# Attention and expert layers in one program: the weight conversion moved into six named slots, and the score chunks in another order

## The chip, the cores and the metric

The kernel runs on one core of one Trainium2 chip. The metric is the device time of one execution in microseconds (us). Engines are named as in the profile: PE (TensorE matmul), PEld (its weight load), DVE (VectorE), ACT (ScalarE), POOL (GpSimd), SP (SyncE, which issues the transfers here).

## What is computed

Attention with a causal softmax and a linear memory, mixed by a gate, and then four matrix products:

```python
scores = scale * np.matmul(q, k.transpose(0, 1, 3, 2))      # B, H, S, D = 4, 8, 576, 64
scores = np.where(causal, -1000000000.0, scores)
a = np.exp(scores - scores.max(-1, keepdims=True))
a /= a.sum(-1, keepdims=True) + 1e-09
local = np.matmul(a, v)
q_p = phi(q)                                                # elu(q) + 1
mem_out = einsum(q_p, M_prev) / (einsum(q_p, z_prev) + 1e-06)
x = (g * mem_out + (1 - g) * local)                         # g = sigmoid(beta); to 2304 x 512
out = ((x @ w1) * (x @ w2) @ w3) @ w_out                    # w* arrive as float64
```

## The kernel before

**Pairs and batches.** Two heads of one batch are a pair; there are 16 pairs, four to a batch. `pair_step(p, F)` does a pair: it walks through the table `ORDER` and calls what each word names. `mt` transposes the memory's query, `t1` to `t5` and `th` transpose the softmax of the pair (`t_mm`, with an eviction by ACT at L265), `mm` and `pv` form the sums of memory and P.V in PSUM (`mem_mm`, `pv_mm`), and `fin` (L292 on ACT, L293 on DVE) copies them out as the high and low half of x. In the same walk the next pair p + 1 is prepared: `ss` makes its scores (`s_all`), `e4` to `e0` exponentiate its chunks (`s_exp`, L215 on ACT), `n4`, `n3`, `n2` multiply them by the gate over the row sum (`s_norm`, L224 on DVE), and `ma`, `mb`, `mc` prepare the memory's query (L137 to L158; L145 and L158 run on POOL). `lv`, `lqn`, `lq` issue loads on SP.

**Chunks.** The 576 rows of scores are five chunks, 0 to 4, of 64, 128, 128, 128, 128 queries; chunk c needs 64, 192, 320, 448 or 576 keys (`KE`). `s_all` writes chunk 4 (512 columns, and 64 more in the next bank) and chunk 3 into four PSUM banks of the pool `ps_t`, and chunks 2 and 1 into the tile `x`, which has one buffer of two banks and is also the tile of P.V's sums. `s_red` (L181, DVE) adds the mask, writes the scores to the tiles `sm` and finds the row maximum. Chunk 0 of both heads is one matmul (L190, `s_mm0`) into a fifth bank of `ps_t`, thus into the first of the four that is free again.

**Filling work.** At each `F` of `ORDER` a slot of filling work is issued: `F.slot()` steps a generator until its share is reached. During the first batch that is `w_gen`, the product of w3 and w_out (L427, 64 matmuls, each of two passes in the trace), whose results are evicted by L432 and L419. From the second batch on it is `moe_gen` of the batch before: L477 (x with w1 and w2, evicted in turn by ACT L483 and DVE L486, then L488 and L489 make the two halves of h) and L497 (h with the product of w3 and w_out).

**Weight conversion.** The weights arrive as 64-bit floats. Forty jobs convert them to 32 bit: load on SP (L388 for w3 and w_out, L303 for w1 and w2), `scale` on ACT (L314), `join` on DVE (L318, L319), and for the last sixteen also `split` (L326 on ACT, L327 on POOL). `conv_tick()` issues one step: the scale of job k, the join of job k - 1, the split of job k - 2. The loads of w1 and w2 share three buffers. `F.slot()` calls it before its filling work, twice per slot in the first 13 slots and once after, where `tick_ok()` allows it:

```python
for _ in range(self.ticks if self.n > SLOTS else 2):
    if tick[0] <= NJ + 1 and tick_ok():
        conv_tick()
```

In the program this gives two ticks before the first slot, 4 to 15 over the six slots before the first pair, 16 to 19 in pair 0, 20 to 25 in pair 1 (22 to 25 of them in the softmax slots at the end), 26 to 31 in pair 2, and 32 to 41 in the first five slots of pair 4. What stands in one engine's queue in the end is set by a scheduler that may move an instruction ahead of others of its engine; instructions under `tc.high_priority` go early.

Of the kernel before, what the change touches and what calls it, by code (L numbers as in the profile page):

```python
# [16 lines left out]

ORDER = (  # L20
    "lv mt t1 F "
    "lqn t2 th F "
    "t3a t3b F "
    "t4a F "
    "t4b t5 F "
    "mm pv ma F "
    "fin F "
    "ss lq mb F "
    "F "
    "e4 mc F "  # L30
    "n4 e3 F "
    "n3 F "
    "e2 e1 e0 n2 F "
).split()


# [5 lines left out]
def attention_moe_kernel(  # L42
# [14 lines left out]
    B, H, D, _, S = qkt.shape  # L57
    DM = H * D
    NF = w12.shape[0]
    NC = DM // 128  # L60
# [127 lines left out]
    def s_mm0(p):  # L188
        x = bank()
        nc.tensor.matmul(x[:, 0:64], lhsT=qd, rhs=raw_t[p][:, 1, 0:64], start=True, stop=True)  # L190
        s_red(p, 0, 0, x[:, 0:64], 0, 64)

    def s_all(p):
        t = raw_t[p]
        lay = []
        for a in range(2):
            lay.append([bank(), bank()])
        xx = ps_x.tile([128, 1024], F32, tag="x", name="sx")
        red = []
        for i, o, c, lo, hi in ((0, 0, 4, 0, 512), (1, 0, 4, 512, 576), (1, 64, 3, 0, 448), (2, 0, 2, 0, 320), (2, 320, 1, 0, 192)):  # L200
            for a in range(2):
                y = xx[:, 512 * a + o:512 * a + o + hi - lo] if i == 2 else lay[a][i][:, o:o + hi - lo]
                r = slice(64 * a, 64 * a + 64)
                nc.tensor.matmul(y, lhsT=t[r, 0, 128 * c - 64:128 * c + 64], rhs=t[r, 1, lo:hi], start=True, stop=True)  # L204
                red.append((c, a, y, lo, hi))
        for c, a, y, lo, hi in red:
            s_red(p, c, a, y, lo, hi, lo == 0)
        s_mm0(p)

    def s_exp(p, c):  # L210
        for a in range(2 if c else 1):
# [165 lines left out]
    def tick_ok():  # L377
        k = tick[0]
        if 12 <= k < 24:
            return w_done[0] >= (k - 8) // 2 - 3  # L380
        return k < 12 or k < limit[0] and (k < 32 or w_done[0] == NF)
# [28 lines left out]
    def conv_upto(k):  # L410
        while tick[0] <= k + (1 if k < 24 else 2):
            conv_tick()
# [103 lines left out]


    class Fill:
        def __init__(self, gen, total, slots, wait=0, lead=1.0, ticks=1):
            self.lead, self.ticks = lead, ticks  # L520
            self.wait = wait
            self.gen, self.total, self.slots = gen, total, slots
            self.spent, self.n, self.live = 0.0, 0, True

        def slot(self):
            self.n += 1
            for _ in range(self.ticks if self.n > SLOTS else 2):
                if tick[0] <= NJ + 1 and tick_ok():
                    conv_tick()
            goal = self.lead * self.total * max(0, self.n - self.wait) / (self.slots - self.wait)  # L530
            while self.live and self.spent < goal:
                self.step()
# [7 lines left out]
        def finish(self):  # L540
            while self.live:
                self.step()

    SLOTS = sum(t[0] == "F" for t in ORDER)

    def pair_step(p, F):
        nx = p + 1 < NP
        ops = dict(
            mt=(1, lambda: mem_t(p)),
            lqn=(nx, lambda: load_qn(p + 1)),  # L550
            lv=(1, lambda: load_v(p)),
            t4a=(1, lambda: t_mm(p, "4a")),
            t4b=(1, lambda: t_mm(p, "4b")),
            t3a=(1, lambda: t_mm(p, "3a")),
            t3b=(1, lambda: t_mm(p, "3b")),
            t2=(1, lambda: t_mm(p, "2")),
            t1=(1, lambda: t_mm(p, "1")),
            th=(1, lambda: t_mm(p, "h")),
            t5=(1, lambda: t_mm(p, "5")),
            ss=(nx, lambda: s_all(p + 1)),  # L560
            e4=(nx, lambda: s_exp(p + 1, 4)),
            e3=(nx, lambda: s_exp(p + 1, 3)),
            e2=(nx, lambda: s_exp(p + 1, 2)),
            e1=(nx, lambda: s_exp(p + 1, 1)),
            e0=(nx, lambda: s_exp(p + 1, 0)),
            n3=(nx, lambda: s_norm(p + 1, 2, 4)),
            n2=(nx, lambda: s_norm(p + 1, 4, 9)),
            n4=(nx, lambda: s_norm(p + 1, 0, 2)),
            lq=(p + 2 < NP, lambda: load_qk(p + 2)),
            mm=(1, lambda: mem_mm(p)),  # L570
            pv=(1, lambda: pv_mm(p)),
            fin=(1, lambda: fin(p)),
            ma=(nx, lambda: mem_a(p + 1)),
            mb=(nx, lambda: mem_b(p + 1)),
            mc=(nx, lambda: mem_c(p + 1)),
        )
        for t in ORDER:
            if t[0] == "F":
                F.slot()
            elif ops[t][0]:  # L580
                ops[t][1]()

# [31 lines left out]
        nc.vector.tensor_copy(out=gis[:, :, 2 * k:2 * k + 2], in_=gp)  # L614
    for a in range(2):
        nc.vector.tensor_copy(out=gis[64 * a:64 * a + 64, :, 8], in_=gp[64 * a:64 * a + 64, :, a])
    s_exp(0, 4)
    conv_tick()
    conv_tick()
    s_norm(0, 0, 2)  # L620
    F.slot()
    for c in (3, 2, 1):
        s_exp(0, c)
        F.slot()
    s_exp(0, 0)
    s_norm(0, 2, 9)
    F.slot()
    load_qk(1)
    mem_a(0)
# [46 lines left out]
```

## Time and profile before

| | us |
|---|---|
| median of 3 runs (lowest, highest) | 582.26 (581.95, 583.43) |
| the profiled execution | 583.85 |
| its span, first to last instruction | 582.1 |
| PE busy in the span | 553.6 |
| DVE, ACT, POOL busy | 277.1, 275.8, 127.4 |

The stages, in us from the span's start: scores of pair 0 to 10; product of w3 and w_out alone to 28; pair 0 to 57, pair 1 to about 81, pair 2 to about 106, pair 3 to 131, then twelve pairs of about 31 us with the expert layers as filling, and the last batch's expert layers alone at the end. The trace is read by engine: a row has the start, the duration, the line, the tiles (out<-in) and, in square brackets, how long the engine stood idle before it and what ended that. A PE that is busy is not always at its full rate: the granted clock has two levels, 1.2 and 2.4 GHz, and a stretch's mean tells how much of it ran at the lower one.

### The profile page before, as it was taken

The numbers are of one execution on the slowest core, as the hardware profiler recorded it, in microseconds if no ns is written. First come the engines' busy times: TensorE is split into PE (matmuls) and PEld (weight loads), VectorE is DVE, ScalarE is ACT, GpSimd is POOL, SyncE is SP. The second block draws the span as 40 slices with busy tenths as digits, with TensorE's granted clock in tenths as the row PEclk, the third lists the DMA queues.
The fourth block names the chain that finished last, engine by engine and source line by source line (L and its number), as shares of the span: only waits on it lengthen the run. The fifth ranks groups of instructions, "written<-read, shape, count | busy, mean of one in ns | idle before, by whom it ended". The sixth has DMA issues, their size and how long they took to land.

```text
span 582.1 us, 9285 instructions
## 1 busy us (share of the span) xinstructions
PE 553.6 (95%) x3440; PEld 436.8 (75%) x3440; DVE 277.1 (48%) x878; ACT 275.8 (47%) x723; POOL 127.4 (22%) x153
## 2 busy tenths in 40 slices
PE   4999879898999999999999999999999999999997
PEld 2354435456888888878887889697979897998995
DVE  6986996837562627262626263524525260111111
ACT  5565876448554445545554555443626363120220
POOL 1101263114613032303230313012130321121220
PEclk9899989798999999999999999999999999999999
DMA  7992554513020211131202120311103000000001
GB/s 288 423 353 91 179 192 147 167 56 102 29 63 21 92 35 58 34 95 42 64 28 83 47 66 29 93 59 37 59 28 101 24 2 1 37 1 20 18 1 54
DMA packets 23069, 48.31 MB, mean 83 GB/s; under 512 B 6896, under 2 KB 13040, under 8 KB 21488
## 3 DMA queue, kind: packets, MB, share of 16 engines
q1 hardware_dynamic: 23024, 47.72, 24.3%
q8 instruction: 27, 0.44, 0.3%
q14 instruction: 18, 0.15, 0.1%
HBM read 43.00 MB, written 4.72 MB: 82 GB/s over the span
## 4 chain that ended last, share of the span: by engine, by line
PE 74%; ACT 6%; DVE 5%; issue 3%; DMA 1%; POOL 1%; SPq 0%; POOLq 0%; ACTq 0%
PE m L477 32%; PE m L497 17%; PE s L234 7%; PE x L281 6%; ACT sm L215 5%; PE s L204 3%; PE m L427 2%; PE x L272 2%; DVE sm L181 1%; PE x L164 1%; DVE wp L319 1%; DVE sm L224 1%; PE sx L204 1%; DMA wst<-w 1%; DVE wp L318 1%
## 5 line engine op out<-in xcount | busy, mean ns | idle before, releaser
L477 PE MATMUL m<-xs,wsp 128*128 128x288 f32 x1536 | 224.5, 300 | 4.0 <-ACT a L483 4.0
L477 PEld LDWEIGHTS m<-xs,wsp 128*128 128x128 f32 x1536 | 208.0, 189 | 6.4 <-ACT a L483 5.4
L489 POOL TENSOR_TENSOR ht<-a,ht 128x288 fp32r<-128x288 f32 (+2 forms) x96 | 57.1, 607 | 246.4 <-ACT ht L488 246.4
L215 ACT ACTIVATE sm<-sm,mx 128x576 f32<-128x576 f32 (+3 forms) x144 | 82.3, 573 | 54.3 <-DVE mx L181 54.3
L497 PE MATMUL m<-wH,ht 128*128 128x512 f32 x288 | 94.0, 395 | 0.0
L486 DVE SCALAR_TENSOR_TENSOR a<-m,a 128x288 f32<-128x288 f32 x64 | 29.1, 455 | 105.6 <-PE m L477 101.8
L265 ACT ACTIVATE pt<-s 128x512 f32<-128x512 f32 (+1 forms) x144 | 63.1, 492 | 28.8 <-PE s L234 28.6
L427 PE MATMUL m<-wo,w3s 128*128 128x512 f32 x128 | 67.3, 662 | 4.6 <-DVE w3s L319 3.8
L234 PE MATMUL s<-ident,sm 128*128 128x128 f32 x448 | 61.9, 274 | 3.6 <-DVE sm L224 3.4
L497 PEld LDWEIGHTS m<-wH,ht 128*128 128x128 f32 x288 | 54.1, 188 | 11.2
L488 ACT ACTIVATE ht<-a 128x288 fp32r<-128x288 f32 (+2 forms) x96 | 31.5, 360 | 65.3 <-DVE a L486 65.3
L234 PEld LDWEIGHTS s<-ident,sm 128*128 128x128 f32 x448 | 52.6, 141 | 10.4 <-DVE sm L224 4.8
L224 DVE TENSOR_SCALAR sm<-sm,sums 128x576 f32<-128x576 f32 (+2 forms) x144 | 56.8, 453 | 0.5
L181 DVE CUSTOM_DVE_ANT_0 sm<-s,mask 128x512 f32<-128x512 f32 (+2 forms) x80 | 44.0, 566 | 27.5 <-PE s L204 27.5
L497 PE MATMUL m<-wL,ht 128*128 128x512 f32 x144 | 56.2, 390 | 0.0
L145 POOL TENSOR_TENSOR e<-qn,z 128x640 f32<-128x640 f32 x16 | 25.8, 1614 | 126.8 <-DVE qn L143 126.8
L483 ACT ACTIVATE a<-m 128x288 f32<-128x288 f32 x64 | 26.1, 407 | 50.3 <-PE m L477 45.0
L427 PEld LDWEIGHTS m<-wo,w3s 128*128 128x128 f32 x128 | 25.0, 212 | 31.6 <-issue 21.5
L281 PEld LDWEIGHTS x<-pt,v 128*64 128x64 f32 x384 | 25.0, 137 | 30.2 <-issue 22.8
L281 PE MATMUL x<-pt,v 128*64 128x448 f32 (+4 forms) x384 | 46.9, 393 | 0.0
L293 DVE TENSOR_TENSOR xs<-x,xs 128x576 fp32r<-128x576 f32 x16 | 12.1, 756 | 64.6 <-ACT xs L292 64.6
L204 PE MATMUL s<-raw 64*128 64x64 f32 (+2 forms) x192 | 37.7, 506 | 4.5 <-DMA raw<-qkt 4.5
(65 smaller groups left out, 474.9 us busy)
## 6 DMA issues: line engine op xcount, KB each, us to landing
raw<-qkt SPq DMA_DIRECT2D x16, 576.0 KB, 3.8
wst<-w3t SPq DMA_DIRECT2D x8, 1024.0 KB, 9.2
wst<-w SPq DMA_DIRECT2D x16, 512.0 KB, 4.8
qn<-qn SPq DMA_DIRECT2D x16, 320.0 KB, 2.9
v<-v SPq DMA_DIRECT2D x32, 160.0 KB, 2.3
out<-o SPq DMA_DIRECT2D x18, 256.0 KB, 2.0
wst<-w_out SPq DMA_DIRECT2D x4, 1024.0 KB, 12.2
z<-z_prev SPq DMA_DIRECT2D x16, 64.0 KB, 2.8
```

The costliest lines, as they stand in the source:

```text
L181: nc.vector.tensor_tensor_reduce(out=sm[a][c][:, lo:hi] if c else sm0[:, 0:64], in0=x, in1=mask[:, S - KE[c] + lo:S - KE[c] + hi] if c els ...
L204: nc.tensor.matmul(y, lhsT=t[r, 0, 128 * c - 64:128 * c + 64], rhs=t[r, 1, lo:hi], start=True, stop=True)
L215: nc.scalar.activation(out=x, in_=x, func=ACTF.Exp, bias=mx, scale=-1.0, accum_out=sums_of(p)[:, k:k + 1])
L224: nc.vector.tensor_scalar(out=x, in0=x, scalar1=sums_of(p)[:, k:k + 1], scalar2=None, op0=ALU.mult)
L234: tr = lambda o, c, a, kc: nc.tensor.transpose(ps[:, o:o + 128], sm[a][c][:, 128 * kc:128 * kc + 128], ident)
L265: nc.scalar.activation(out=d, in_=s, func=ACTF.Copy)
L281: nc.tensor.matmul(x[64 * a:64 * a + 64, 384 + q0:384 + q1], lhsT=vv[:, a, kc], rhs=pt[:, a, o:o + q1 - q0], start=False, stop=(q0 == 0 or ...
L427: nc.tensor.matmul(ps, lhsT=w[:, 128 * kc:128 * kc + 128], rhs=wo[:, 512 * (kc % 2):512 * (kc % 2) + 512], start=(kc == 0), stop=(kc == 7))
L477: nc.tensor.matmul(ps[:, 0:U], lhsT=w[:, i, x, j], rhs=x_t[NC * b + j][:, xx, U * u:U * u + U], start=(k == 0), stop=(k == 11))
L488: nc.scalar.activation(out=hbuf(f, 0)[:, p:p + c], in_=a[:, o:o + c], func=ACTF.Copy)
L489: nc.gpsimd.tensor_tensor(out=hbuf(f, 1)[:, p:p + c], in0=a[:, o:o + c], in1=f32(hbuf(f, 0)[:, p:p + c]), op=ALU.subtract)
L497: nc.tensor.matmul(ps, lhsT=hbuf(f, a)[:, p:p + 128], rhs=b[f], start=(k == 0), stop=(k == 23))
```

## The change

`F.slot()` no longer ticks. A word `c` stands in `ORDER` ahead of the first six `F` (transposes and P.V), and there one tick is issued in pairs 0 to 3 and two after. The softmax of the next pair goes from the small chunks to the large one: chunks 2, 1, 0 are exponentiated and normalised first, then 3, then 4. `s_all` puts chunks 2 and 1 in the first bank of each head, chunk 3 and the last 64 columns of chunk 4 in the second, and the 512 columns of chunk 4 in the tile `x`; chunk 0's matmul follows the reductions of chunks 2 and 1 in the program. Before the first pair the order is the same, with ticks 0 to 11. The new places of the ticks are: 12 to 17 in pair 0, 18 to 21 in pair 1, 22 to 27 in pair 2, 28 to 31 in pair 3, 32 to 41 in pair 4, the last as before. The slots of filling work and what each slot steps are the same.

```diff
-    "lv mt t1 F "
+    "lv mt t1 c F "
...
-    "e4 mc F "
-    "n4 e3 F "
-    "n3 F "
-    "e2 e1 e0 n2 F "
+    "e2 e1 e0 mc F "
+    "n2 e3 F "
+    "e4 n3 F "
+    "n4 F "
...
-        for i, o, c, lo, hi in ((0, 0, 4, 0, 512), (1, 0, 4, 512, 576), (1, 64, 3, 0, 448), (2, 0, 2, 0, 320), (2, 320, 1, 0, 192)):
+        for i, o, c, lo, hi in ((0, 0, 2, 0, 320), (0, 320, 1, 0, 192), (1, 0, 3, 0, 448), (2, 0, 4, 0, 512), (1, 448, 4, 512, 576)):
...
-        for c, a, y, lo, hi in red:
+        for k, (c, a, y, lo, hi) in enumerate(red):
             s_red(p, c, a, y, lo, hi, lo == 0)
-        s_mm0(p)
+            if k == 3:
+                s_mm0(p)
...
-            for _ in range(self.ticks if self.n > SLOTS else 2):
-                if tick[0] <= NJ + 1 and tick_ok():
-                    conv_tick()
...
+    def try_tick():
+        if tick[0] <= NJ + 1 and tick_ok():
+            conv_tick()
...
-            if t[0] == "F":
+            if t == "F":
                 F.slot()
+            elif t == "c":
+                for _ in range(1 if p < NC else 2):
+                    try_tick()
...
+    s_exp(0, 2)
+    conv_tick()
+    s_exp(0, 1)
+    conv_tick()
+    s_exp(0, 0)
+    s_norm(0, 4, 9)
+    conv_upto(4)
+    F.slot()
+    s_exp(0, 3)
+    try_tick()
+    try_tick()
+    F.slot()
+    s_norm(0, 2, 4)
     s_exp(0, 4)
-    conv_tick()
-    conv_tick()
+    try_tick()
+    try_tick()
+    F.slot()
     s_norm(0, 0, 2)
+    try_tick()
+    try_tick()
     F.slot()
-    for c in (3, 2, 1):
-        s_exp(0, c)
-        F.slot()
-    s_exp(0, 0)
-    s_norm(0, 2, 9)
-    F.slot()
```

Three places in the engines' queues follow. In all, `sm_107` is chunk 0, `sm_108` to `sm_111` are chunks 1 to 4 of the pair's first head and `sm_112` to `sm_115` those of its second; lines of after are two or so higher than those of before.

DVE before, behind the reductions of pair 4's scores; `sums` are the row sums:

```order
L219 SCALAR_TENSOR_TENSOR sums<-sums,gis 128x2 x2
L220 RECIPROCAL sums<-sums 128x2 x2
L224 TENSOR_SCALAR sm_111<-sm_111,sums 128x576
L224 TENSOR_SCALAR sm_115<-sm_115,sums 128x576
L224 TENSOR_SCALAR sm_110<-sm_110,sums 128x448
L224 TENSOR_SCALAR sm_114<-sm_114,sums 128x448
L219 SCALAR_TENSOR_TENSOR sums<-sums,gis 128x5
L220 RECIPROCAL sums<-sums 128x5
L224 TENSOR_SCALAR sm_109<-sm_109,sums 128x320
L224 TENSOR_SCALAR sm_113<-sm_113,sums 128x320
L224 TENSOR_SCALAR sm_108<-sm_108,sums 128x192
L224 TENSOR_SCALAR sm_112<-sm_112,sums 128x192
```

DVE after, at the same place:

```order
L221 SCALAR_TENSOR_TENSOR sums<-sums,gis 128x5
L221 SCALAR_TENSOR_TENSOR sums<-sums,gis 128x2
L222 RECIPROCAL sums<-sums 128x5
L222 RECIPROCAL sums<-sums 128x2
L226 TENSOR_SCALAR sm_109<-sm_109,sums 128x320
L226 TENSOR_SCALAR sm_113<-sm_113,sums 128x320
L226 TENSOR_SCALAR sm_108<-sm_108,sums 128x192
L226 TENSOR_SCALAR sm_112<-sm_112,sums 128x192
L226 TENSOR_SCALAR sm_107<-sm_107,sums 128x64
L226 TENSOR_SCALAR sm_110<-sm_110,sums 128x448
L226 TENSOR_SCALAR sm_114<-sm_114,sums 128x448
```

The multiplications of chunks 2 and 1, which the first transposes read, moved from behind those of chunks 4 and 3 to the front.

DVE before, between the first and the second large reduction of pair 2's scores; `wp` are tiles of converted w1 and w2, L293 is the copy that frees the tile `x` of pair 1:

```order
L318 TENSOR_SCALAR wp<-wp 128x512
L319 SCALAR_TENSOR_TENSOR wp<-wst,wp 128x512
L143 SCALAR_TENSOR_TENSOR qn<-qn,e 128x640
L318 TENSOR_SCALAR wp<-wp 128x512
L319 SCALAR_TENSOR_TENSOR wp<-wst,wp 128x512
L293 TENSOR_TENSOR xs<-x,xs 128x576
L181 ISA sm_115,mx<-s,mask 128x512
```

DVE after, up to the first reduction of pair 2's scores:

```order
L320 TENSOR_SCALAR wp<-wp 128x512
L321 SCALAR_TENSOR_TENSOR wp<-wst,wp 128x512
L144 SCALAR_TENSOR_TENSOR qn<-qn,e 128x640
L320 TENSOR_SCALAR wp<-wp 128x512
L321 SCALAR_TENSOR_TENSOR wp<-wst,wp 128x512
L151 TENSOR_REDUCE n<-e 128x10
L295 TENSOR_TENSOR xs<-x,xs 128x576
L182 ISA sm_109,mx<-s,mask 128x320
```

The copy L293 (L295 after) still stands behind two conversions, and now also behind the reduction L150 (L151 after), which reads what POOL writes.

ACT before, at the softmax of pair 5; `a` and `ht` belong to the expert layers:

```order
L488 ACTIVATE ht<-a 128x288
L215 ACTIVATE sm_111,sums<-sm_111,mx 128x576
L215 ACTIVATE sm_110,sums<-sm_110,mx 128x448
L215 ACTIVATE sm_115,sums<-sm_115,mx 128x576
L215 ACTIVATE sm_114,sums<-sm_114,mx 128x448
L215 ACTIVATE sm_109,sums<-sm_109,mx 128x320
L483 ACTIVATE a<-m 128x288
L215 ACTIVATE sm_113,sums<-sm_113,mx 128x320
```

ACT after, at the same place:

```order
L490 ACTIVATE ht<-a 128x288
L217 ACTIVATE sm_109,sums<-sm_109,mx 128x320
L217 ACTIVATE sm_113,sums<-sm_113,mx 128x320
L217 ACTIVATE sm_108,sums<-sm_108,mx 128x192
L217 ACTIVATE sm_112,sums<-sm_112,mx 128x192
L217 ACTIVATE sm_107,sums<-sm_107,mx 128x64
L485 ACTIVATE a<-m 128x288
L217 ACTIVATE sm_110,sums<-sm_110,mx 128x448
```

The eviction L483 (L485 after) stands behind five exponentials in both, but of the large chunks before and of the small ones after.

## Rows read from the trace of the kernel before

**Rows 1.** The page's first part: busy time, share of span, instructions.

```profile
PE 553.6 (95%) x3440; PEld 436.8 (75%) x3440; DVE 277.1 (48%) x878; ACT 275.8 (47%) x723; POOL 127.4 (22%) x153
```

**Rows 2.** PE's waits, 0 to 143 us, then to the end: total, times, longest.

```profile
PE sx L204 <- DVE xs L293: 4.0, 3, 3.5
PE m L427 <- DVE w3s L319: 3.8, 2, 3.5
PE s L234 <- DVE sm L224: 3.4, 2, 2.3
...
PE x L164 <- POOL qn L158: 1.9, 2, 1.0
...
PE m L477 <- ACT a L483: 4.0, 6, 0.7
```

**Rows 3.** Stretches: busy PE, PEld, DVE, ACT, POOL, then granted clock, DMA.

```profile
81.00:100.00 19.00, 18.89 (x88) 10.46 (x86) 13.99 (x46) 14.21 (x37) 6.37 (x5) 0.91 0.51 158
100.00:112.00 12.00, 9.52 (x30) 4.55 (x30) 11.09 (x39) 6.69 (x21) 1.77 (x2) 0.72 0.70 216
112.00:143.00 31.00, 28.69 (x137) 17.14 (x136) 18.96 (x57) 17.81 (x43) 7.03 (x6) 0.94 0.22 64
143.00:480.00 337.00, 333.01 (x2315) 283.12 (x2314) 154.88 (x536) 168.16 (x463) 78.35 (x95) 1.00 0.17 52
```

**Rows 4.** PE's timeline at pairs 1 to 4: start, duration, what, idle before.

```profile
66.95 1.33 PE L234 MATMUL s<-ident,sm 128*128 128x128 f32 x10 [1.09 <-DVE sm L224]
...
70.94 1.12 PE L204 MATMUL s<-raw 64*128 64x512 f32 x2
...
74.63 2.10 PE L204 MATMUL s<-raw 64*128 64x512 f32 x10
80.19 1.13 PE L204 MATMUL sx<-raw 64*128 64x320 f32 x8 [3.46 <-DVE xs L293]
...
100.01 2.10 PE L204 MATMUL s<-raw 64*128 64x512 f32 x12
...
105.74 0.69 PE L190 MATMUL s<-raw,qd 128*128 128x64 f32 x2 [2.28 <-DVE mx L181]
...
131.34 5.37 PE L427 MATMUL m<-wo,w3s 128*128 128x512 f32 x12
...
139.57 1.11 PE L234 MATMUL s<-ident,sm 128*128 128x128 f32 x4 [2.31 <-DVE sm L224]
```

**Rows 5.** DVE's timeline around the scores of pairs 2 and 4.

```profile
70.60 0.69 DVE L319 SCALAR_TENSOR_TENSOR wp<-wst,wp 128x512 uint32<-128x512 uint32 x1
...
76.06 1.74 DVE L318 TENSOR_SCALAR wp<-wp 128x512 uint32<-128x512 uint32 x1 [1.17 <-ACT wp L314]
77.84 1.63 DVE L319 SCALAR_TENSOR_TENSOR wp<-wst,wp 128x512 uint32<-128x512 uint32 x1
79.39 0.74 DVE L293 TENSOR_TENSOR xs<-x,xs 128x576 fp32r<-128x576 f32 x1
...
84.51 0.22 DVE L219 SCALAR_TENSOR_TENSOR sums<-sums,gis 128x2 f32<-128x2 f32 x2
...
133.58 0.42 DVE L219 SCALAR_TENSOR_TENSOR sums<-sums,gis 128x2 f32<-128x2 f32 x2
```

**Rows 6.** DVE's timeline: the five multiplications of chunks 2 to 0, twice.

```profile
113.34 1.30 DVE L224 TENSOR_SCALAR sm<-sm,sums 128x320 f32<-128x320 f32 x5
...
136.57 3.33 DVE L224 TENSOR_SCALAR sm<-sm,sums 128x320 f32<-128x320 f32 x5
```

**Rows 7.** POOL's timeline at the second of these.

```profile
136.71 2.69 POOL L327 TENSOR_TENSOR wsp<-wp,wsp 128x512 fp32r<-128x512 f32 x2 [11.66 <-ACT wsp L326]
```

**Rows 8.** ACT's timeline at the softmax of pair 5, first exponential and eviction.

```profile
161.44 0.78 ACT L215 ACTIVATE sm<-sm,mx 128x576 f32<-128x576 f32 x1 [2.39 <-DVE mx L181]
...
164.83 0.39 ACT L483 ACTIVATE a<-m 128x288 f32<-128x288 f32 x1
```

**Rows 9.** PE's timeline at the same place.

```profile
165.27 1.99 PE L477 MATMUL m<-xs,wsp 128*128 128x288 f32 x13 [0.75 <-ACT a L483]
```

More of the change, by code (lines that the diff above doesn't have):

```diff
@@ L20 @@
 ORDER = (
-    "lv mt t1 F "
[L22 to L26, printed above, removed]
+    "lv mt t1 c F "
+    "lqn t2 th c F "
+    "t3a t3b c F "
+    "t4a c F "
+    "t4b t5 c F "
+    "mm pv ma c F "
     "fin F "
@@ L518, in attention_moe_kernel, with __init__ @@
     class Fill:
-        def __init__(self, gen, total, slots, wait=0, lead=1.0, ticks=1):
-            self.lead, self.ticks = lead, ticks
+        def __init__(self, gen, total, slots, wait=0, lead=1.0):
+            self.lead = lead
             self.wait = wait
```

## The prediction, made before the changed kernel ran

> **What bounds the kernel now.** I read the page's first part, then PE's waits in two stretches, then a table of stretches with the clock, and only then the timelines at each wait. PE is busy 553.6 us of a span of 582.1 [rows 1], so the end is PE's end, and anything the change does to DVE, ACT or POOL counts only through a wait of PE, through PE's clock, or through matmuls that run alone where two could run together. From 143 us on PE waits 4.0 us in all, six times, each time for the eviction L483 [rows 2]; between 143 and 480 us the granted clock is 1.00 [rows 3]. The rest of the loss lies ahead of 143 us, where the weight conversion shares DVE, ACT and POOL with the softmax. The waits there that the change can touch are 4.0 (the tile x, L293), 3.4 (the first transposes wait for the multiplication L224), 1.9 (L164 waits for POOL) [rows 2] and 2.3 us (L190 waits for a bank) [rows 4]. The clock adds to this: means of 0.91 over 19 us, 0.72 over 12 and 0.94 over 31 [rows 3] are mixtures of the two levels, and cost 0.09 x 19 + 0.28 x 12 + 0.06 x 31 = 1.7 + 3.4 + 1.9 = 7.0 us of full-speed work; the waits of 3.46, 2.28 and 2.31 us [rows 4] lie ahead of or in these stretches. So 11.6 us of waits, 7.0 of clock and 4.0 in the expert stage are what there is to win; a gain much beyond 22 us is excluded.
>
> The sum is made against the profiled execution, 583.85 us. The median of the runs is 582.26, 1.6 lower; the predicted time is for such a median.
>
> **The change part by part.** No instruction of weight is added or removed: the same matmuls, reductions, exponentials and conversions run, in other places. What moves:
>
> *Before the first pair and in pair 0.* The multiplications of chunks 2, 1 and 0 and one more join of w_out now stand ahead of the second converted half of w3 on DVE. A join L319 takes 0.69 us [rows 5], an L318 no longer, so the second L427, which waited for 0.3 us (3.8 less 3.5) [rows 2], waits up to 1.4 us more, while PE runs at 1.2 GHz. Behind it PE catches up in part at a later wait, L164 for POOL, of 1.0 us at most [rows 2]. I take +0.7 us, between -0.5 (the first transposes now fill a gap) and +3.
>
> *The transposes' wait in pair 1.* 1.09 us [rows 4] were spent until chunk 1 was multiplied, behind chunks 4 and 3. They now come first on DVE. The wait for L164 stays, since its chain (L143, POOL, L150, POOL) stays. With the 0.3 us at pair 1's tile x (4.0 less 3.46 and 0.2) [rows 2, 4] I take -1.4, between -2 and +1.
>
> *A score pair that ran apart.* In pair 2 the chunk-4 matmul of one head ran alone at 70.94, for 1.12 us, and the other ten passes then took 2.10; where all twelve run together they take 2.10 as well [rows 4]. The two heads use different rows of the array at once, so the matmul that ran apart cost about 1.0 us. In the new order of PE's queue the scores of pair 2 stand together behind P.V: -1.0.
>
> *Pair 2's wait for the tile x.* The 3.46 us [rows 4] come from DVE: L293 stood behind two joins that took 1.74 and 1.63 us with 1.17 us of waiting for ACT ahead of them [rows 5], where an undisturbed join takes 0.69 [rows 5]; L293 ended 80.13 - 74.63 = 5.5 us after P.V. In the new queue two joins and now L150 still stand ahead of it. ACT has three short steps behind P.V (a split, a scale, L292; each no longer than the 0.78 us of an exponential of 576 columns [rows 8]), some 2.0 us, then L293 for 0.74; with 0.6 us for the chain through POOL the tile is free 3.3 us after P.V. PE has 2.0 us of scores of chunks 2, 1 and 3 to do (960 columns against the 1024 that took 2.10 [rows 4]). A wait of 1.3 us is left: -2.2, between -3.5 and 0. The clock fell behind the wait of 3.46 us; the 1.7 us between 81 and 100 us [rows 3] are its price. With a wait of a third of the length I take it as gone: -1.7, between -1.7 and 0.
>
> *Pair 2's first transposes, new.* Before, these did not wait. After, DVE does from L293's end: eleven reductions (80.13 to 84.51, 4.4 us with an L150 of 0.8 among them [rows 5], thus 3.6 to 4.4), two pairs of joins (four steps of up to 0.69, 2.5), L419 (0.7, as a join), small steps (0.6), three multiplications of the five that take 1.30 [rows 6] (0.8): 8.2 to 9.0. PE meanwhile has 1.1 us of chunk 4, L190 0.3, seven L427 at 5.37 / 6 = 0.9 [rows 4], five transposes 0.5: 8.2. I take +0.7, between 0 and +2, or +3.7 with a fall of the clock.
>
> What POOL does to DVE is part of this term. Five multiplications took 3.33 instead of 1.30 us [rows 6] while two L327 ran for 2.69 us [rows 7]: 0.75 us per us of POOL, so one L327 met here costs 1.0 us. The Trainium skill (SBUF — State Buffer, section "SBUF: two separate sides") says that DVE and GpSimd take a shared pair of ports as an exclusive lock for a whole instruction and the loser blocks fully; by that one L327 would cost its whole 1.35 us and the predicted time would be 0.3 us higher. The trace agrees in kind, with less than the full block.
>
> *Pair 3's wait for a bank.* L190 waited 2.28 us [rows 4] because DVE came late to the scores, behind joins. It now needs only chunks 2 and 1 of one head, but in DVE's new queue these stand behind L293 and three more conversion steps that pass through ACT and POOL. I take -0.3, between -2.5 and +1.5, and leave the clock behind it as it is (3.4 us at most to win [rows 3]).
>
> *Pair 4's first transposes.* They waited 2.31 us [rows 4]: DVE multiplied chunks 4 and 3 first, then met the two L327. In the new queue chunks 2 and 1 follow the row sums at once: from 133.58 + 0.4 = 134.0 [rows 5], 1.3 us, done at 135.3, or 137.3 with both L327 in it [rows 6, 7]. PE is ready at 139.57 - 2.31 = 137.26 [rows 4], since six L427 (5.37 us, from 131.34) cover it. So -2.3; and the 1.9 us of clock up to 143 us [rows 3] go with it, of which I take 1.7. Between -1 and -4.2 in all. What is late next is chunk 4, which is read four slots later.
>
> *The expert stage.* L483 stood at 164.83 behind five exponentials that began at 161.44 [rows 8], 3.39 us with 2368 columns, and PE waited 0.75 us for it [rows 9]. The five ahead of it now have 1088 columns and start earlier, as the first reduction is of 320 columns and not 512. Even if half of each exponential's time were fixed, 3.39 shrinks to 2.5 us, more than 0.75 earlier. The waits are 4.0 us in six [rows 2]; where a chunk-3 exponential still stands ahead one may stay. I take -3.4, between -4.0 and -1.5.
>
> The tick words change nothing after pair 4. The product of w3 and w_out has the same 64 matmuls in the same slots; only four of them wait longer for their place on PE, until pair 2.
>
> Sum: 0.7 - 1.4 - 1.0 - 2.2 - 1.7 + 0.7 - 0.3 - 2.3 - 1.7 - 3.4 = -12.6; 583.85 - 12.6 = 571.25, and 1.6 less for a median: 569.7 us.
>
> **The rivals.**
>
> 1. *The conversions keep PE waiting in pairs 1 and 2.* L293 stays behind joins and POOL, so nothing of pair 2's 3.46 us, its clock or pair 1's wait is won; what happens after 112 us holds. For it: two joins stand ahead of L293 as before. Against it: the 1.17 us in which ACT was late [rows 5] should be gone with fewer conversions in pair 1. Time: only +0.7 - 1.0 + 0.7 - 0.3 - 4.0 - 3.4 = -7.3, thus 575.0.
>
> 2. *Pair 3's bank wait closes too.* If DVE reaches chunks 2 and 1 early, 2.28 us and the 3.4 us of clock behind it go, and pair 2's new wait does not appear: 569.7 - 2.0 - 3.4 - 0.7 = 563.6.
>
> 3. *Slower: late weights.* Ticks 12 to 15 move from ahead of pair 0 into it, one per slot. If a converted half of w3 arrives later than the L427 that reads it, PE waits one chain (scale, two joins), 0.7 + 0.7 + 0.7 = 2.1 us, for each of the eight ticks from 12 to 19: 16.8 us, against 12.6 won: 586.5. It decides from six such waits on. For it: L427 waited for w3 twice already [rows 2]. Against it: each scale still stands at least a slot ahead of its reader in the program, and L427 waited for w3 only at the start.
>
> A fourth case, that the wins and new waits cancel within a microsecond or so, has no place of its own and a small chance.
>
> **How the numbers follow.** Forecast 0.56, rival 1 0.22, rival 2 0.10, rival 3 0.08, cancelling 0.04. The likeliest gives 569.7. The range takes in rivals 1 and 2 with the bounds of the two largest terms (pair 2's tile and clock, and the expert stage, some 4 us): 562 to 579; the tenth to an eighth left out lies almost all above. Faster by over 0.3% (1.7 us, about what a measurement of this kernel can tell from no change) has 0.88, within it 0.04, slower 0.08.
>
> **What would show it.** In the changed kernel's waits: no "s L234 <- DVE sm" at pair 4 and no clock below 1.00 from there; "m L477 <- ACT a" below 1 us in total; "sx L204 <- DVE xs" near 1.3 us in pair 2; a new wait of L234 in pair 2 below 2 us; "s L190" still near 2 us. It would be wrong if L427 waits for w3s beyond the first, if pair 1 or 2 shows a longer gap than 3.5 us, or if the clock falls in a stretch where it had been 1.00.

## The result and the profile after

The changed kernel takes **571.97 us** (median of 4 runs, 571.37 to 572.48) against 582.11 for the kernel before on the same chip (581.50 to 583.43): a ratio of 0.9822, with a 95% interval of 0.9802 to 0.9843. The predicted time was 569.7, in a range of 562 to 579.

| | before | after |
|---|---|---|
| the profiled execution, us | 583.85 | 571.37 |
| its span | 582.1 | 569.6 |
| PE busy in the span | 553.6 | 545.4 |

The spans differ by 12.5 us, the medians by 10.1. The profiled execution of before was 1.7 us above the median of its four runs; that of after is 0.6 below its own.

The first part of the page of after, which answers [rows 1]:

```profile
PE 545.4 (96%) x3440; PEld 436.4 (77%) x3440; DVE 279.4 (49%) x880; ACT 277.5 (49%) x723; POOL 126.6 (22%) x153
```

Lines of after are two or so higher than before: L429 is L427, L479 is L477, L485 is L483, L295 is L293, L191 is L190, L205 is L204, L236 is L234, L329 is L327, L320 and L321 are L318 and L319. PE's waits of after from 0 to 143 us (total, times, longest), as [rows 2]; behind 143 us the same view is empty, where before had 4.0 us in six waits for L483:

```profile
PE sx L205 <- DVE xs L295: 5.5, 2, 3.2
PE s L205 <- DMA raw<-qkt: 4.5, 1, 4.5
PE m L429 <- DVE w3s L321: 3.8, 1, 3.8
PE m L429 <- DVE wo L321: 1.7, 2, 1.1
PE s L191 <- DVE mx L182: 1.6, 1, 1.6
PE x L165 <- POOL qn L159: 1.4, 2, 0.7
PE m L479 <- DVE wL L421: 1.3, 1, 1.3
...
```

So the wait for the tile x did not shrink in all: it is 5.5 us where it was 4.0. PE's timeline of after shows where these stand (pairs 2, 3, 3, 4, 4), as [rows 4]:

```profile
71.87 1.13 PE L205 MATMUL sx<-raw 64*128 64x512 f32 x4 [2.32 <-DVE xs L295]
...
100.02 1.76 PE L205 MATMUL sx<-raw 64*128 64x512 f32 x4 [3.19 <-DVE xs L295]
...
103.73 0.69 PE L191 MATMUL s<-raw,qd 128*128 128x64 f32 x2 [1.63 <-DVE mx L182]
...
133.63 0.60 PE L236 MATMUL s<-ident,sm 128*128 128x128 f32 x4
...
137.87 1.87 PE L479 MATMUL m<-xs,wsp 128*128 128x288 f32 x12 [1.28 <-DVE wL L421]
```

Pair 2's wait for x fell from 3.46 to 2.32; pair 3 has a new one of 3.19; pair 4's first transposes wait no more (2.31 before); and the first expert product has a new wait of 1.28 us. Stretches of after with their clock (columns as in [rows 3]):

```profile
73.10:76.50 3.40, 3.40 (x8) 1.85 (x7) 3.40 (x16) 3.37 (x12) 1.93 (x2) 0.50 0.38 110
100.40:107.20 6.80, 5.17 (x14) 2.62 (x11) 5.49 (x17) 3.60 (x12) 1.02 (x1) 0.50 0.70 209
107.20:143.00 35.80, 34.52 (x187) 22.35 (x187) 24.88 (x78) 25.22 (x64) 10.42 (x8) 1.00 0.34 103
```

PE still ran at 1.2 GHz for 3.4 us behind pair 2's wait and for 6.8 us behind pair 3's, as before; the third such stretch of before, 3.4 us at pair 4, is gone.

**Where the time went.** The matmul of chunk 0 (L190, now L191) is a mark that every pair has. Its start in both traces, and the difference with the L427 that were done up to there made equal (25 of after against 28 at pair 1, 31 against 35 at pair 2, the same number from pair 3 on; 0.86 us from the start of one to that of the next):

| to L190 of pair | before | after | difference at equal work | of this stretch | predicted for it |
|---|---|---|---|---|---|
| 1 | 54.83 | 52.39 | +0.1 | +0.1 | +0.7 |
| 2 | 81.25 | 73.10 | -4.7 | -4.8 | -1.4 - 1.0 - 2.2 = -4.6 |
| 3 | 105.74 | 103.73 | -2.0 | **+2.7** | -1.7 + 0.7 - 0.3 = **-1.3** |
| 4 | 131.07 | 127.60 | -3.5 | -1.5 | 0 |
| 5 | 161.63 | 155.69 | -5.9 | -2.5 | -2.3 - 1.7 = -4.0 |
| the end of the span | 582.1 | 569.6 | -12.5 | **-6.6** | **-3.4** |

The sum, -12.5 against -12.6, is better than its terms. Two rows failed by more than 3 us, in opposite directions (+4.0 at pair 3, -3.2 at the end). That the total agrees so closely is luck.

### The profile page after: what moved, and what is told of

Its sections match the earlier page's. It is cut to its first block, busy times and chain, and to the rows that moved or that the text cites. A ratio compares the mean times of both kernels' runs of the same rounds, so it can differ in the third digit from the quotient of the medians.

```text
span 569.6 us, 9266 instructions
## 1 busy us (share of the span) xinstructions
PE 545.4 (96%) x3440; PEld 436.4 (77%) x3440; DVE 279.4 (49%) x880; ACT 277.5 (49%) x723; POOL 126.6 (22%) x153
## 4 chain that ended last, share of the span: by engine, by line
PE 82%; DVE 8%; ACT 4%; issue 2%; POOL 2%; DMA 2%; SPq 0%; POOLq 0%; DVEq 0%
PE m L479 36%; PE m L499 18%; PE x L283 7%; PE s L236 7%; PE s L205 4%; PE m L429 4%; PE x L274 2%; PE sx L205 2%; DVE sm L226 2%; PE x L165 1%; DVE sm L182 1%; POOL wsp L329 1%; DMA wst<-w_out 1%; ACT pt L267 1%; PE s L191 1%
## 5 line engine op out<-in xcount | busy, mean ns | idle before, releaser
L479 PE MATMUL m<-xs,wsp 128*128 128x288 f32 x1536 | 221.6, 299 | 1.3 <-DVE wL L421 1.3
L479 PEld LDWEIGHTS m<-xs,wsp 128*128 128x128 f32 x1536 | 206.7, 188 | 2.3 <-DVE wL L421 1.5
L217 ACT ACTIVATE sm<-sm,mx 128x320 f32<-128x320 f32 (+2 forms) x144 | 82.7, 576 | 39.5 <-DVE mx L182 38.5
L488 DVE SCALAR_TENSOR_TENSOR a<-m,a 128x288 f32<-128x288 f32 x64 | 29.1, 455 | 99.1 <-PE m L479 94.7
L429 PE MATMUL m<-wo,w3s 128*128 128x512 f32 x128 | 65.5, 647 | 6.2 <-DVE w3s L321 3.8
L490 ACT ACTIVATE ht<-a 128x288 fp32r<-128x288 f32 (+2 forms) x96 | 31.5, 360 | 63.2 <-DVE a L488 63.1
L236 PE MATMUL s<-ident,sm 128*128 128x128 f32 x448 | 61.7, 273 | 0.0
L236 PEld LDWEIGHTS s<-ident,sm 128*128 128x128 f32 x448 | 52.7, 140 | 7.2 <-issue 5.8
L226 DVE TENSOR_SCALAR sm<-sm,sums 128x320 f32<-128x320 f32 (+2 forms) x144 | 57.1, 457 | 0.4
L182 DVE CUSTOM_DVE_ANT_0 sm<-s,mask 128x320 f32<-128x320 f32 (+3 forms) x112 | 44.4, 448 | 24.4 <-PE s L205 24.3
L146 POOL TENSOR_TENSOR e<-qn,z 128x640 f32<-128x640 f32 x16 | 25.3, 1581 | 136.3 <-DVE qn L144 112.9
L485 ACT ACTIVATE a<-m 128x288 f32<-128x288 f32 x64 | 26.1, 408 | 50.7 <-PE m L479 45.4
L429 PEld LDWEIGHTS m<-wo,w3s 128*128 128x128 f32 x128 | 24.4, 209 | 31.3 <-issue 20.0
L295 DVE TENSOR_TENSOR xs<-x,xs 128x576 fp32r<-128x576 f32 x16 | 12.1, 756 | 66.6 <-ACT xs L294 66.6
L205 PE MATMUL s<-raw 64*128 64x320 f32 (+3 forms) x256 | 38.3, 414 | 4.5 <-DMA raw<-qkt 4.5
```

The costliest lines, as they stand in the source:

```text
L182: nc.vector.tensor_tensor_reduce(out=sm[a][c][:, lo:hi] if c else sm0[:, 0:64], in0=x, in1=mask[:, S - KE[c] + lo:S - KE[c] + hi] if c els ...
L217: nc.scalar.activation(out=x, in_=x, func=ACTF.Exp, bias=mx, scale=-1.0, accum_out=sums_of(p)[:, k:k + 1])
L226: nc.vector.tensor_scalar(out=x, in0=x, scalar1=sums_of(p)[:, k:k + 1], scalar2=None, op0=ALU.mult)
L236: tr = lambda o, c, a, kc: nc.tensor.transpose(ps[:, o:o + 128], sm[a][c][:, 128 * kc:128 * kc + 128], ident)
L429: nc.tensor.matmul(ps, lhsT=w[:, 128 * kc:128 * kc + 128], rhs=wo[:, 512 * (kc % 2):512 * (kc % 2) + 512], start=(kc == 0), stop=(kc == 7))
L479: nc.tensor.matmul(ps[:, 0:U], lhsT=w[:, i, x, j], rhs=x_t[NC * b + j][:, xx, U * u:U * u + U], start=(k == 0), stop=(k == 11))
```

## The experiments

All ratios are against the kernel before, run beside it on the same chip; the theories and rivals are those written down before each run.

**The halves of the change.** e1 is the kernel before with the words of the softmax and the new `s_all`, and the ticks as they were:

```diff
-    "e4 mc F "
-    "n4 e3 F "
-    "n3 F "
-    "e2 e1 e0 n2 F "
+    "e2 e1 e0 mc F "
+    "n2 e3 F "
+    "e4 n3 F "
+    "n4 F "
...
+        for i, o, c, lo, hi in ((0, 0, 2, 0, 320), (0, 320, 1, 0, 192), (1, 0, 3, 0, 448), (2, 0, 4, 0, 512), (1, 448, 4, 512, 576)):
...
+            if k == 3:
+                s_mm0(p)
```

> The kernel before with the new score layout and the new order of the softmax, and the conversion's ticks where they were. Theory (the order of the chunks brings the gain): the six waits for L483 in the expert stage and pair 4's wait for the first transposes are gone, so it keeps the 6.6 us won behind pair 4 and the 2.4 us won in pair 4: 571 to 575 us. Rival (taking the conversions out of the softmax slots brings it): 579 to 583 us, with waits for L483 left.

Measured: 572.2 us, ratio 0.9823 (0.9798 to 0.9847), the whole gain.

e2 is the other half, ticks only:

```diff
-    "lv mt t1 F "
+    "lv mt t1 c F "
...
-    "mm pv ma F "
+    "mm pv ma c F "
```

> The kernel before with the ticks ahead of the first six slots of a pair (0 to 11 before the first pair, as in the changed kernel), and the old score layout and order of the softmax. Theory: nothing changes in the expert stage, six waits for L483 of 4.0 us in all, pair 4's first transposes still wait; 579 to 584 us. Rival: 571 to 575 us.

Measured: 585.53 us, ratio 1.0044 (1.0027 to 1.0061): slower. Its trace has seven waits for L483 (4.5 us in all, the eviction is L484 there), and the first transposes wait more often than in before:

```profile
PE s L235 <- DVE sm L225: 6.6, 4, 3.4
...
PE m L478 <- ACT a L484: 4.5, 7, 0.8
```

So the half that the change's name begins with brings nothing. Its time lies 1.5 us above the theory's range.

**Within the softmax half.** e3 has the new `s_all` alone, e4 the new order of words alone.

> The kernel before with the new places and the new order of the score matmuls and reductions alone; chunk 4 is still exponentiated first in the program. Theory: both halves of the softmax change are needed, since chunk 4's exponentials now begin when its reductions end, last; L483 and the first transposes wait as long as before or longer: 581 to 588 us. Rival (the layout alone frees the early chunks, the scheduler does the rest): 573 to 577 us.

> The kernel before with the new order of exponentials and multiplications alone; chunks 2 and 1 are still reduced last. Theory: the multiplications of chunks 2 and 1 come first on DVE, so pair 4's first transposes wait less, but the small exponentials start 2 to 3 us later than in the changed kernel, so L483 still waits in the expert stage (3 us or more in all): 576 to 582 us. Rival (the order of the multiplications is all that counts): 571 to 575 us.

Measured: e3 572.8 us, ratio 0.9836 (0.9811 to 0.9861); e4 582.35, ratio 0.9995 (0.9983 to 1.0006). My expectation for e3 fell: I had taken the words as what orders the exponentials. In e3 they stand in the program as before, and yet the scheduler puts chunks 2, 1 and 0 first on ACT, as in after; in e4 the words name chunk 2 first, and ACT's queue is that of before. PE's first transposes wait as long in e4 as in before (2.5 us at the longest against 2.3), which I had expected to shrink. The scheduler goes by what is ready, and `s_all` decides that.

It has two parts: the banks (with the order of the score matmuls, which follows them) and the order in which the reductions are written. e5 changes the second alone, e6 the first alone:

```diff
# e5, old banks
+        for k, (c, a, y, lo, hi) in enumerate(red[6:] + red[4:6] + red[:4]):
             s_red(p, c, a, y, lo, hi, lo == 0)
+            if k == 3:
+                s_mm0(p)
# e6, new banks, the old order of reductions and s_mm0 at the end
+        for c, a, y, lo, hi in red[6:] + red[4:6] + red[:4]:
```

> The kernel before with one edit: DVE's reductions (and chunk 0's matmul) are written in the new order, chunks 2 and 1 first, while the scores stay in their old banks and the order of the matmuls, the words and the ticks stay. Theory 1 (the places of the chunks in PSUM carry the gain, as chunks 2 and 1 in the tile x can't be ready before L293 and the scheduler goes by that): the exponentials still begin with the large chunks, L477's waits for L483 stay near 4 us, 580 to 584 us. Rival (the order in which the reductions are written carries it): those waits are gone and the time is 572 to 576.

> The kernel before with the other half: new places and the new order of the score matmuls, but the reductions written in the old order (chunk 4, chunk 3, then 2, 1, and chunk 0 at the end). Theory 1 (places carry the gain): 572 to 577 us; chunks 2 and 1 are exponentiated first, and at most one of two L483 per softmax stands behind large chunks, so L477's waits for L483 are below 2.5 us. Rival (written order of the reductions): 580 to 584, with waits for L483 of about 4.

Measured: e5 583.81 us, ratio 1.0013 (0.9998 to 1.0029), with 3.5 us of waits for L483 left; e6 573.8, ratio 0.9842 (0.9811 to 0.9873). The banks carry it. In before chunks 2 and 1 lay in the tile `x`, which PE may write only when L293 has read P.V's sums; whatever the program says of them, they come last. ACT's timeline of e6 at the softmax of pair 5 has them first, and two L483 in it:

```profile
155.21 0.56 ACT L215 ACTIVATE sm<-sm,mx 128x320 f32<-128x320 f32 x1 [0.75 <-DVE mx L181]
...
157.73 0.41 ACT L483 ACTIVATE a<-m 128x288 f32<-128x288 f32 x1 [0.45 <-PE m L477]
158.04 0.77 ACT L215 ACTIVATE sm<-sm,mx 128x576 f32<-128x576 f32 x1
...
161.20 0.39 ACT L483 ACTIVATE a<-m 128x288 f32<-128x288 f32 x1
```

The first now stands behind four short exponentials and waits for PE, not PE for it; the second stands behind the four long ones, and PE has no wait for it either. From 143 us on no wait of PE is left in e6, as in after.

The traces of all runs but e9 bear this out. From the matmul of chunk 0 of pair 5 to the end of the span it takes 420.3 to 420.8 us with the old banks (before, e2, e4, e5) and 413.9 to 414.2 with the new ones (after and all the others). What the experiments below win, they win ahead of that mark.

**What keeps PE waiting in pairs 2 and 3.** In after's DVE timeline ahead of pair 3's wait of 3.19 us, single steps are far longer than the 0.42 us of an undisturbed L320, the 0.69 of an L321 and the 0.17 of an L152:

```profile
92.11 1.28 DVE L152 TENSOR_SCALAR n<-n 128x10 f32<-128x10 f32 x1
...
94.10 1.45 DVE L320 TENSOR_SCALAR wp<-wp 128x512 uint32<-128x512 uint32 x1 [0.26 <-ACT wp L316]
95.59 0.69 DVE L321 SCALAR_TENSOR_TENSOR wp<-wst,wp 128x512 uint32<-128x512 uint32 x1
97.53 1.04 DVE L320 TENSOR_SCALAR wp<-wp 128x512 uint32<-128x512 uint32 x1 [1.25 <-ACT wp L316]
...
99.21 0.75 DVE L295 TENSOR_TENSOR xs<-x,xs 128x576 fp32r<-128x576 f32 x1
...
100.33 1.63 DVE L321 SCALAR_TENSOR_TENSOR wp<-wst,wp 128x512 uint32<-128x512 uint32 x1
```

POOL's timeline of after in the same stretch:

```profile
92.09 1.27 POOL L329 TENSOR_TENSOR wsp<-wp,wsp 128x512 fp32r<-128x512 f32 x1 [1.76 <-ACT wsp L328]
94.01 1.26 POOL L159 TENSOR_TENSOR qn<-qn,n 128x640 f32<-128x640 f32 x1 [0.66 <-DVE n L157]
97.02 1.26 POOL L329 TENSOR_TENSOR wsp<-wp,wsp 128x512 fp32r<-128x512 f32 x1 [1.75 <-ACT wsp L328]
100.04 1.38 POOL L329 TENSOR_TENSOR wsp<-wp,wsp 128x512 fp32r<-128x512 f32 x1 [1.75 <-ACT wsp L328]
```

Each of the four long DVE steps begins while a POOL step runs, and ends 0.03 to 0.54 us after it (92.11 + 1.28 = 93.39 against 92.09 + 1.27 = 93.36), less than its own undisturbed length. Ahead of 143 us, nine DVE steps of after are longer than the median of their line and shape by 7.9 us in all beside an L329, and six more by 6.8 us beside POOL's two steps of the memory's query, L146 and L159. Not every step that meets POOL is longer. In the whole trace of after, the evictions L488 (eight of them) and L421, reductions of scores (L182), L151 and L222 also began beside one of these POOL steps, and took their usual time. An L488 on DVE that lies wholly inside a POOL step, and that step:

```profile
153.73 0.45 DVE L488 SCALAR_TENSOR_TENSOR a<-m,a 128x288 f32<-128x288 f32 x1
```

```profile
153.31 1.26 POOL L159 TENSOR_TENSOR qn<-qn,n 128x640 f32<-128x640 f32 x1 [1.69 <-DVE n L157]
```

L488, L421 and L182 read an operand from PSUM (the tiles `m`, `s` and `sx`); the steps that stood still (L144, L152, L221, L226, L320, L321) have all their tiles in SBUF.

POOL is in the way a second time: the two buffers of tag `o` come free only behind L329, so L316 on ACT, and the join behind it, can wait for POOL. ACT's timeline of after has such a wait ahead of the join at 94.10:

```profile
93.39 0.68 ACT L316 ACTIVATE wp<-wst 128x512 f32<-128x512 f32 x1 [1.38 <-POOL wsp L329]
```

The 1.25 us above are not one: that L316 ran at 96.85, right behind the split's L328, which had waited for DVE's own join.

e7 is after with one line changed, and PE's order is the same word for word:

```diff
-            nc.gpsimd.tensor_tensor(out=dl(), in0=box["p"], in1=f32(dh()), op=ALU.subtract)
+            nc.vector.tensor_tensor(out=dl(), in0=box["p"], in1=f32(dh()), op=ALU.subtract)
```

> The changed kernel with one edit: the subtraction of split (L329, 16 of about 1.3 us on POOL) runs on DVE; PE's order is the same word for word. Theory 1 (what keeps PE waiting in pairs 2 and 3 is DVE's joins stretched by POOL's L329, 0.69 to between 1.0 and 1.9 us, and the chain through POOL): joins fall back to 0.7 us, L329 on DVE takes about 0.7, pair 3's wait of 3.2 us for the tile x falls below 2, and the time is 569 to 571. Rival (it is the number of steps in DVE's queue ahead of L295): the additional 0.7 us each make the waits as long or longer, 572 to 575.

Measured: 567.62 us, ratio 0.9744 (0.9712 to 0.9776), although DVE has 16 steps more. The same two waits for x in its PE timeline, and the L329 on DVE:

```profile
72.17 1.13 PE L205 MATMUL sx<-raw 64*128 64x512 f32 x4 [1.83 <-DVE xs L295]
...
97.37 1.13 PE L205 MATMUL sx<-raw 64*128 64x512 f32 x4 [1.21 <-DVE xs L295]
...
99.79 0.60 PE L191 MATMUL s<-raw,qd 128*128 128x64 f32 x2 [1.12 <-DVE mx L182]
```

```profile
91.63 0.69 DVE L329 TENSOR_TENSOR wsp<-wp,wsp 128x512 fp32r<-128x512 f32 x1 [0.18 <-ACT wsp L328]
```

Pair 3's wait for x fell from 3.19 to 1.21, and L191 of pair 3 starts at 99.79 where it was 103.73. Theory 1's figure for the wait held and the time came out below its range (569 to 571). DVE's busy time hardly changed (279.4 to 280.2 us), though it took over 16 steps of 0.69 us: what it no longer lost beside POOL about paid for them. How much of the gain is the stalled steps and how much the shorter chain (0.69 us instead of 1.27, and the buffers sooner free), e7 doesn't separate.

e8 makes the same edit on e1 (the softmax half with the old ticks), e9 on the kernel before.

> Only the softmax half of the change (old ticks, new words and places), and the subtraction of split on DVE. That half alone took 572.2 us. Theory 1 (POOL stretches DVE): 569 to 571 us, with a wait of L235 for the multiplications of pairs 1 to 4 below 1 us where it was 2.5. Rival (number of DVE steps): 572 to 575.

> The kernel before with one edit: the subtraction of split runs on DVE. Theory 1 (DVE's steps stand still while a POOL step runs, whatever the order of chunks; in the trace of before seven steps of DVE ahead of 143 us were longer by 5.2 us in all beside an L327): 576 to 580 us, with pair 2's wait for the tile x below 2.5 us where it was 3.5 and pair 4's first transposes below 1 where it was 2.3. Rival (moving the split is worth something only with the new places): 581 to 584.

Measured: e8 566.36 us, ratio 0.9722 (0.9689 to 0.9755); e9 578.56, ratio 0.9898 (0.9866 to 0.9931). No trace of e9 is read here, so its waits stay untested. POOL was in DVE's way in before too; the edit is worth 1.0% there and 1.0% on top of the softmax half. e8 came out below theory 1's range, but the wait for the multiplications, which was to fall below 1 us, is still 2.0 (2.5 in e1). In e8 the clock is full from 20 us on:

```profile
20.00:143.00 123.00, 113.88 (x566) 65.08 (x567) 101.59 (x279) 84.20 (x195) 19.52 (x13) 1.00 0.52 183
```

e10 also moves POOL's two steps of the memory's query in e8 to DVE, e11 only the second of them:

```diff
# e10 and, the second line alone, e11
+        nc.vector.tensor_tensor(out=e, in0=t, in1=zb, op=ALU.mult)
...
+        nc.vector.tensor_tensor(out=tv, in0=tv, in1=n.to_broadcast([128, 10, D]), op=ALU.mult)
```

> The softmax half with split on DVE (566.4 us), and the two steps of the memory's query that run on POOL (L145 of 1.7 and L158 of 1.3 us, one each per pair) on DVE too. Theory 1 (they stall DVE as L327 did; 7.8 us of stretched steps ahead of 143 us in that kernel's trace): 563.5 to 565.5, and no DVE step ahead of 143 us longer than 1.3 times its median. Rival (DVE now gets 32 steps of some 0.8 us, 26 us in all, which delay L293 and the reductions in every pair): 566 to 571, with new waits of PE from 143 us on.

> As the one before, but only the second of the two steps (L158) on DVE; L145 stays on POOL. Theory 1: 564.5 to 566, about half of what both give. Rival: 566 to 569.

Measured: e10 **559.98 us**, ratio 0.9592 (0.9567 to 0.9617), the fastest of all; e11 564.64, ratio 0.9670 (0.9643 to 0.9697). Theory 1 holds in sign: e11 is in its range, and e10 gave more than it allowed (563.5 at the least). e10 is 24.2 us below the kernel before (584.2 beside it), and the prediction had called a gain much beyond 22 us excluded, from the printed waits and the clock. The page's first part of e10 has DVE at 298.0 and POOL at 61.9:

```profile
PE 541.2 (97%) x3440; PEld 434.5 (78%) x3440; DVE 298.0 (53%) x926; ACT 278.5 (50%) x723; POOL 61.9 (11%) x105
```

DVE is busy for 18.6 us more than in after, and POOL for 64.7 less, so the gain is not a saving of DVE's time. Two DVE steps ahead of 143 us are still over 1.3 times their median, where theory 1 had none (an L319 and an L320, beside L490, a POOL step of the expert layers). The memory's query also has a shorter chain now: its two steps take 0.82 and 0.92 us on DVE in the mean, and took at least 1.54 and 1.25 on POOL in after. What this brings and what the end of the stalls brings, no run separates. PE's waits of e10 from 0 to 143 us have none for the tile x:

```profile
PE m L428 <- DVE w3s L320: 4.7, 1, 4.7
PE s L204 <- DMA raw<-qkt: 4.4, 1, 4.4
PE s L235 <- DVE sm L225: 1.2, 1, 1.2
PE s L190 <- DVE mx L181: 1.2, 1, 1.2
PE x L164 <- DVE qn L158: 1.0, 2, 0.8
PE s L235 <- ACT pt L266: 0.4, 1, 0.4
```

Last, e12 is the whole changed kernel with all three POOL steps moved; it differs from e10 by the places of the ticks alone.

> The whole changed kernel, with the split's subtraction and both POOL steps of the memory's query on DVE; against the softmax half with the same moves (559.98 us) it differs by the places of the ticks alone. Theory 1 (the tick half is worth nothing, with or without POOL in DVE's way): 559 to 561.5 us. Rival (the tick half is worth something once DVE's steps have one length): 556 to 558.5.

Measured: 562.95 us, ratio 0.9656 (0.9634 to 0.9679), above e10 with no overlap of the intervals. Both theories missed: the tick half costs some 3 us here. In e12 pair 3's L191 waits 2.04 us and pair 3's first transposes 2.38 (1.18 and 1.19 in e10), and 3.4 us behind the second run at 1.2 GHz.

## Why the prediction was right, and where it was not

**The expert stage: the right mechanism, half the size.** The prediction read the waits of [rows 2], 4.0 us in six, as all that could be won, and took 3.4 of it; 6.6 us were won. The eviction moved as forecast: five exponentials ahead of it still, but from 154.61 to 157.07, 2.46 us, where the prediction had 2.5 for its 3.39. ACT's timeline of after:

```profile
154.61 0.56 ACT L217 ACTIVATE sm<-sm,mx 128x320 f32<-128x320 f32 x1
...
157.07 0.41 ACT L485 ACTIVATE a<-m 128x288 f32<-128x288 f32 x1
```

What was mis-sized is, in part, the price of a wait. PE's timeline of before ahead of [rows 9], and of after at the same place:

```profile
161.88 2.64 PE L477 MATMUL m<-xs,wsp 128*128 128x288 f32 x18
```

```profile
155.93 4.24 PE L479 MATMUL m<-xs,wsp 128*128 128x288 f32 x30
```

Thirty passes take 4.24 us and 18 take 2.64, so one more costs (4.24 - 2.64) / 12 = 0.133 us. The last two of the 18 passes, in a view of before that begins later:

```profile
164.09 0.43 PE L477 MATMUL m<-xs,wsp 128*128 128x288 f32 x2
```

Behind these the next could start at 164.09 + 2 x 0.133 = 164.36; it started at 165.27 [rows 9]. That is 0.91 us lost, where the view shows 0.75: a wait is counted from the modelled end of a matmul, and back-to-back passes overlap. The six waits, taken in this way, cost 4.95 us. So 3.4 became 4.0 because no wait stayed, 4.95 because each costs more than it shows, and the other 1.6 us of the 6.6 stand in no wait that the view prints. By the starts of the passes, 0.9 of these lie between other L477 and 0.5 ahead of the matmul of chunk 0; why is open.

**Pair 3: the step that failed.** The prediction gave pair 3 a term for the bank alone (-0.3), since its tile x had cost 0.2 us before, and so took what is won up to pair 2 as kept. The wait of 3.19 us for the tile x came there, with the bank's 1.63 (2.28 before) behind it. It also kept in the sum that the 1.7 us of clock behind pair 2's wait would go, with a wait of 1.3 us left. The wait left was 2.32, and PE ran at 1.2 GHz for 3.4 us behind it as before. Together: +2.7 instead of -1.3.

The places of the ticks decide which wait it is, and not whether the time is lost: in e1, with the old ticks, the wait for x is 1.19 us, but the matmul of chunk 0 of pair 3 starts at 105.13, later than the 103.73 of after, with other waits ahead of it. In the eight traces in which POOL has its old work (before, after, e1 to e6) this matmul starts between 102.7 and 108.0, with the same 45 L427 done. The one line of e7 leaves pair 2's mark where it was (73.39 against 73.10) and moves pair 3's to 99.79; in e8 it is 99.27, in e10 93.93. Against before, at equal work, the stretch from mark to mark costs 2.7 us more in after and 1.5 us less in e7: POOL's subtraction is what made PE lose there again what it had won. Rival 1 (conversions keep PE waiting) named the mechanism for pairs 1 and 2; it happened in part in pair 2, and in pair 3, where no rival had it.

Two readings behind the 1.3 us were wrong. It allowed 0.6 us for the chain through POOL, which no row gave; in after the L146 there took 1.65 us and stretched the join beside it to 1.91, as DVE's timeline shows. And the 1.17 us of [rows 5] that the prediction put down to a late ACT began with a load, as ACT's timeline of before shows:

```profile
68.51 1.91 DVE L321 SCALAR_TENSOR_TENSOR wp<-wst,wp 128x512 uint32<-128x512 uint32 x1
```

```profile
75.36 0.67 ACT L314 ACTIVATE wp<-wst 128x512 f32<-128x512 f32 x1 [1.24 <-DMA wst<-w]
```

**The weight of POOL.** The prediction had 0.75 us of DVE lost per us of POOL and put one L327 (1.0 us) into one term. The rows of pair 3 above show the price by the step: 1.03 us of 1.26 for the L320 at 94.10, 1.11 of 1.27 for the L152 at 92.11. The size was near; what the prediction missed was how many steps meet, and that POOL decides the result: moving its steps won 4 us in e7, and 6 from e8 to e10. The Trainium skill (SBUF — State Buffer, section "SBUF: two separate sides") says that of a GpSimd op and a DVE op in a 2-port perf mode, or with two SBUF inputs against a GpSimd op that reads SBUF, the one that starts first gets the shared pair of ports for the whole instruction and "the other fully blocks". The rows of after agree with the block and with its condition: the steps with two inputs in SBUF (L144, L221, L321) ended only after the POOL step, and those with one input in PSUM (L421, L488) ran on. Which of the steps with one input run in such a mode, no trace here tells. The mean of [rows 6, 7] had hidden the full block, since it counted DVE's time between two POOL steps too.

**What held.** To L190 of pair 2, -4.8 against -4.6, though the wait for x shrank to 2.32 and not to 1.3, so that another part was better than forecast; which one isn't settled. The first transposes of pair 2 (+0.7, in the next stretch) did not wait. At pair 4 the transposes' 2.31 us and the clock behind them went as forecast; the new wait of 1.28 us took some of that back. It stands behind L421, which DVE reached at 137.13 behind nine multiplications, three of which POOL had stretched by 1.0 us each; DVE's timeline of after:

```profile
130.84 4.09 DVE L226 TENSOR_SCALAR sm<-sm,sums 128x320 f32<-128x320 f32 x7
...
135.24 1.97 DVE L226 TENSOR_SCALAR sm<-sm,sums 128x576 f32<-128x576 f32 x2
137.13 0.68 DVE L421 SCALAR_TENSOR_TENSOR wL<-m,wH 128x512 fp32r<-128x512 f32 x1
```

Between pairs 3 and 4 nothing was forecast, and the 1.5 us there are no gain of their own: in before the 6.8 us at 1.2 GHz lie behind pair 3's mark, and in after the first 3.3 of them (100.40 to 103.73) lie ahead of it, in pair 3's row. The twelve L427 passes behind the mark took 6.86 us instead of 8.27.

Rival 3 (late weights) did not come: L429 waited for w3s once, 3.8 us, at the start. That the ticks would change nothing after pair 4 held; that they would help ahead of it did not (e1 and after, 572.2 and 571.97, are the same; e2 and e12 are slower than without). The expert stage's step gave as its reason that the first reduction is of 320 columns; it is so because of the banks and not because of the order in which the reductions are written (e5, e6).

**From the sum to the median.** 1.6 us were taken off because the profiled execution of before lay that much above the median of the three runs known then. The one of after lay 0.6 below. Those 2.2 us are the whole difference of 569.7 and 571.97.

## What to carry to other kernels

Where two engines work side by side, look beside each step that is longer than its median for a step of the other engine; here moving POOL's steps to the busier DVE won 12 us (572.2 to 559.98), more than the change itself, although DVE was then busy for longer (276.4 us in e1, 298.0 in e10). Where a scheduler orders the queues, a dependence (which bank a result is written to, and who must read that bank first) can move work where the order of words doesn't: here the banks brought 573.8 us and the words 582.35. Ask of time won in one stretch whether the next keeps it. Price a repeated wait on PE by the start of the next matmul against the pace of those before it, not by the wait that a view prints.

## What the runs showed of the hardware

Some DVE steps that begin beside a POOL step end only when that has ended: 0.17 us became 1.28 (L152), 0.42 became 1.45 (L320, rows of pair 3 above). Others run on beside it: 0.45 us for an L488 inside a POOL step of 1.26. In after the steps that stood still had all their tiles in SBUF; of those that ran on, L182, L421 and L488 read PSUM, and L151 and L222 are a reduction and a reciprocal.

The same subtraction took 1.27 us on POOL and 0.69 on DVE. Where it met one of the stalled steps (nine in after, 7.9 us ahead of 143 us) it cost DVE 0.9 us of stall on average.

PE's clock fell to 1.2 GHz for 3.4 or 6.8 us behind a single wait of 2.32 (pair 2 of after) and of 3.19 us (pair 3), and in e7 behind two of 1.21 and 1.12 with little work between, yet not behind the single 1.83 us of e7's pair 2 or the 2.04 of e12's pair 3. No rule is drawn from these few.
